# Attention feeding an ELU feed-forward layer: the Tile scheduler's order of the engines exchanged for one written by hand

## The chip, the cores and the metric

The kernel runs on one core of a Trainium2 chip. The metric is the device time of one execution in microseconds (us), the median of several runs. The core has five engines with an instruction stream each: TensorE (PE) multiplies matrices and writes to PSUM, VectorE (DVE) and ScalarE (ACT) work element by element, GpSimd (POOL) does too and issues transfers from a software queue, and SyncE (SP) issues transfers from a hardware queue. An engine works its stream in order; engines wait for each other by semaphores.

## The reference, cut to what matters

There are 8 batches of 8 heads, 576 queries and keys of 64 elements, and 16 beacon keys and values per batch in front of them. All inputs and the output are float32.

```python
k_all = np.concatenate([beacon_k, k], axis=2)      # 16 + 576 = 592 keys
v_all = np.concatenate([beacon_v, v], axis=2)
scores = scale * np.matmul(q, k_all.transpose(0, 1, 3, 2))
scores = np.where(causal, -1000000000.0, scores)   # beacons are seen by all
a = np.exp(scores - scores.max(-1, keepdims=True))
a /= a.sum(-1, keepdims=True) + 1e-09
attn = np.matmul(a, v_all)                         # (8, 8, 576, 64)
x = attn.transpose(0, 2, 1, 3).reshape(4608, 512)
h = x @ w_in                                       # 512 -> 2048
g = np.where(h > 0.0, h, np.exp(np.minimum(h, 0.0)) - 1.0)
out = g @ w_out                                    # 2048 -> 512
```

## The kernel before

Attention goes by batch and by pair of heads (`emit_pair`, 32 of them). Queries and keys arrive as bfloat16 with the token on the partition, are transposed on PE (`tq`, `tk`) and copied by ACT to `qT` and `kT`, in which the two heads of a pair lie on partitions 0 to 63 and 64 to 127. For each of five chunks of 128 keys and each head, PE computes a strip of scores with the keys on the partitions (`stp`), for the queries from `ilo` on that may see the chunk: 576, 464, 336, 208 and 80 columns. ACT takes the exponential to `et` (10 activations for a pair), and DVE multiplies the diagonal block with a triangle. Then PE sums over the keys, for query columns 0 to 511 and 512 to 575 apart: values times weights to `u_ps` and, with a block of ones, the row sums to `l_ps`. ACT forms the reciprocal of the row sums as exp(-ln(l)), in two activations (`rl`, L243 and L244), and DVE multiplies it in (`xallT`, L245).

The feed-forward layer goes by tiles of 512 tokens, nine of them (`gen_moe_tile`). FFN1 has 16 chunks of four matmuls of 512 columns (`hps`); each chunk goes through an exponential on ACT (`e_sb`), a maximum on DVE (`r_sb`) and a combination on DVE (`gt`). FFN2 has four output blocks of 16 matmuls (`ops`), each copied by DVE to `osb` and stored by SP. A tile is cut into eight steps; after each pair of heads up to three steps of the tile at hand are put into the program, if its tokens are complete. What is left when the attention is done runs behind it, with other PSUM buffers.

Loads: q and k come by casting transfers that POOL issues, one for each 128 tokens, with 256-byte rows (64 float32). v comes uncast by SP and is cast by POOL. The two weight matrices come uncast by SP in 32 pieces and are cast by DVE. The Tile framework orders the instructions of each engine by priority and puts in the semaphores.

Of the kernel before, what the change touches and what calls it, by code (L numbers as in the profile page):

```python
# [12 lines left out]
ALU = mybir.AluOpType  # L14


def _ceildiv(a, b):
    return (a + b - 1) // b
# [3 lines left out]
def kernel(  # L22
# [57 lines left out]
    konst = ctx.enter_context(tc.tile_pool(name="konst", bufs=1))  # L80
    big = ctx.enter_context(tc.tile_pool(name="big", bufs=1))
    astage = ctx.enter_context(tc.tile_pool(name="astage", bufs=2))
    attn = ctx.enter_context(tc.tile_pool(name="attn", bufs=2))
    melt = ctx.enter_context(tc.tile_pool(name="melt", bufs=3))
    gpool = ctx.enter_context(tc.tile_pool(name="gpool", bufs=18))
    opool = ctx.enter_context(tc.tile_pool(name="opool", bufs=2))

    ident = konst.tile([P, P], FP32)
    make_identity(nc, ident)
    identb = konst.tile([P, P], BF16)  # L90
    make_identity(nc, identb)
    triu32 = konst.tile([P, P], FP32)
    nc.gpsimd.memset(triu32, 1.0)
    nc.gpsimd.affine_select(
        out=triu32,
        in_=triu32,
        compare_op=ALU.is_ge,
        fill=0.0,
        base=0,
        pattern=[[1, P]],  # L100
        channel_multiplier=-1,
    )
# [5 lines left out]
    w_out16 = big.tile([P, NFC, DM], FP16)

    def load_batch_stage(b):  # L110
        qst = astage.tile([P, NQT, H, D], BF16, tag="qst")
        kst = astage.tile([P, NKC, H, D], BF16, tag="kst")
        vst32 = astage.tile([P, NKC, H, D], FP32, tag="vst32", bufs=1)
        for sti in range(NQT):
            n = q_tsz[sti]
            nc.gpsimd.dma_start(  # L116
                out=qst[0:n, sti, :, :],
                in_=q[b, :, P * sti:P * sti + n, :].rearrange("h s d -> s h d"),
            )
        for (src, bsrc, dst, eng) in ((k, beacon_k, kst, nc.gpsimd), (v, beacon_v, vst32, nc.sync)):  # L120
            eng.dma_start(
                out=dst[0:NB, 0, :, :],
                in_=bsrc[b, :, :, :].rearrange("h n d -> n h d"),
            )
            for jc in range(NKC):
                lo = max(0, P * jc - NB)
                r0 = NB if jc == 0 else 0
                n = kc_sz[jc] - r0
                eng.dma_start(  # L129
                    out=dst[r0:r0 + n, jc, :, :],  # L130
                    in_=src[b, :, lo:lo + n, :].rearrange("h s d -> s h d"),
                )
        v16 = astage.tile([P, NKC, H, 2, D], FP16, tag="v16")
        for jc in range(NKC):
            n = kc_sz[jc]
            nc.gpsimd.tensor_copy(out=v16[0:n, jc, :, 0, :], in_=vst32[0:n, jc, :, :])
        nc.gpsimd.memset(v16[:, :, :, 1, :], 1.0)
        v16f = v16.rearrange("p nkc h two d -> p nkc (h two d)")
        return qst, kst, v16f

    def emit_weights():
        CH = 512
        with tc.tile_pool(name="wstage", bufs=3) as wstage:
            for cc in range(NCC):
                for fo in range(0, DF, CH):
                    wst = wstage.tile([P, CH], FP32, tag="w_st")
                    nc.sync.dma_start(out=wst, in_=moe_w_in[cc * P:(cc + 1) * P, fo:fo + CH])
                    nc.vector.tensor_copy(out=w_in16[:, cc, fo:fo + CH], in_=wst)  # L148
            for fc in range(NFC):
                wst = wstage.tile([P, DM], FP32, tag="w_st")  # L150
                nc.sync.dma_start(out=wst, in_=moe_w_out[fc * P:(fc + 1) * P, :])
                nc.vector.tensor_copy(out=w_out16[:, fc, :], in_=wst)
# [97 lines left out]
    def gen_moe_tile(psum, tt):  # L250
        gts = []
        for fc in range(NFC):
# [18 lines left out]
            if fc % 4 == 3:  # L271
                yield
# [20 lines left out]
    with tc.tile_pool(name="psumI", bufs=1, space=bass.MemoryType.PSUM) as psumI:  # L293
# [3 lines left out]
        for b in range(B):  # L297
            if b + 1 < B:
                stages[b + 1] = load_batch_stage(b + 1)
# [50 lines left out]
```

## Time and profile before

| what | value |
|---|---|
| median of 3 runs | 537.46 us (536.59 to 537.99) |
| span of the profiled execution | 535.9 us |
| PE busy | 472.3 us, 88% of the span, 3392 matmuls |
| DVE busy | 315.4 us, 59% |
| ACT busy | 288.0 us, 54% |
| POOL busy | 117.7 us, 22% |
| moved by DMA | 37.66 MB in 124649 packets, mean 70 GB/s |

The profile gives the profiled execution by its span alone, the time from its first to its last instruction; what lies around the span is read from the timed runs, whose median is 1.6 us above it. Matmuls are pipelined and their ends are modelled, so the busy time of PE counts overlaps and the start-to-start distance of two matmuls tells their cost. In a row of the timeline the first number is the start, the second the time to the end of the last instruction of the row; a bracket gives the idle time of the engine before it and what ended it. The transfer sizes of the casting queue count the bytes written.

### The profile page before, as it was taken

The page shows a single profiled execution, that of the slowest core. Times are in us where ns is not written, and L with a number is a line of the kernel's source. Part 1 is how long each engine was busy: PE and PEld are TensorE (multiplying, and loading weights), DVE is VectorE, ACT ScalarE, POOL GpSimd, SP SyncE. Part 2 cuts the span into 40 slices and gives each one's busy share as a digit, 9 for nine tenths or more (in the row PEclk, how much of TensorE's full clock was granted, in tenths as well). Part 3 has the DMA queues.
Part 4 walks back from the last instruction along what each step waited for, and adds up shares of the span by engine and source line. Part 5 has one row for each costly group of instructions (what it writes and reads, how often), then busy time and mean ns, then how long its engine had stood idle before and what let it go on. Part 6 is the DMA issues. An engine that isn't in the chain of part 4 may idle for free.

```text
span 535.9 us, 8863 instructions
## 1 busy us (share of the span) xinstructions
PE 472.3 (88%) x3392; PEld 210.9 (39%) x3392; DVE 315.4 (59%) x741; ACT 288.0 (54%) x657; POOL 117.7 (22%) x146
## 2 busy tenths in 40 slices
PE   0268898999999999999999999999999999689997
PEld 0023333444444444444444444444444444234442
DVE  0533336667566656665666646665665466449594
ACT  0224555678357836783577457844775577224150
POOL 8912064025300630064006300640000000000000
PEclk9999999999999999999999999999999999999999
DMA  9995596319510941094109420911001100110202
GB/s 172 184 199 148 148 203 146 63 11 81 131 39 1 91 125 45 2 91 117 55 0 91 100 72 1 89 41 41 1 0 40 40 2 1 39 40 0 80 0 79
DMA packets 124649, 37.66 MB, mean 70 GB/s; under 512 B 115904, under 2 KB 115904, under 8 KB 124608
## 3 DMA queue, kind: packets, MB, share of 16 engines
q0 software_dynamic: 76160, 9.57, 28.1%
q1 hardware_dynamic: 48448, 27.53, 18.5%
q8 instruction: 26, 0.43, 0.3%
q14 instruction: 15, 0.12, 0.1%
HBM read 37.22 MB, written 9.44 MB: 87 GB/s over the span
## 4 chain that ended last, share of the span: by engine, by line
PE 70%; ACT 14%; DVE 7%; issue 4%; DMA 3%; SPq 1%; DVEq 0%
PE hps L255 22%; PE ops L276 21%; PE stp L191 9%; PE u_ps L232 7%; PE l_ps L237 7%; ACT e_sb L263 6%; DMA wst<-in_moe_w_in_dram 3%; ACT rl L243 3%; DVE r_sb L265 2%; PE tq L159 2%; PE tk L170 1%; DVE w_in_96 L148 1%; ACT kT L176 1%; DVE osb L284 1%; SPq L129 1%
## 5 line engine op out<-in xcount | busy, mean ns | idle before, releaser
L276 PE MATMUL ops<-w_out_97,gt 128*128 128x512 f16 x576 | 147.8, 380 | 4.2 <-DVE osb L284 2.3
L265 DVE TENSOR_SCALAR r_sb<-hps 128x512 f16<-128x512 f32 x144 | 98.1, 689 | 88.8 <-ACT e_sb L263 88.8
L263 ACT ACTIVATE e_sb<-hps 128x512 f32<-128x512 f32 x144 | 86.2, 599 | 91.6 <-PE hps L255 69.1
L267 DVE SCALAR_TENSOR_TENSOR gt<-e_sb,r_sb 128x512 f16<-128x512 f32 x144 | 98.9, 695 | 1.3
L191 PE MATMUL stp<-qT,kT 64*128 64x64 bf16 (+6 forms) x640 | 81.0, 253 | 12.1 <-ACT kT L176 2.0
L276 PEld LDWEIGHTS <-gt 128*128 128x128 f16 x576 | 55.2, 97 | 71.6 <-issue 6.7
L116 POOL DMA_DIRECT2D qst<-in_q_dram x40 | 33.8, 865 | 176.2 <-PE tq L159 143.3
L255 PEld LDWEIGHTS <-w_in_96 128*128 128x128 f16 x576 | 49.5, 98 | 57.7 <-issue 12.2
L191 PEld LDWEIGHTS <-kT 64*128 64x128 bf16 (+1 forms) x640 | 32.1, 100 | 94.0 <-issue 83.2
L284 DVE COPY osb<-ops 128x512 f32<-128x512 f32 x36 | 24.7, 690 | 59.5 <-PE ops L276 59.4
L255 PE MATMUL hps<-xallT_92,w_in_96 128*128 128x512 f16 x144 | 56.0, 389 | 4.0 <-DVE r_sb L265 2.7
L255 PE MATMUL hps<-xallT_94,w_in_96 128*128 128x512 f16 x144 | 55.3, 384 | 0.0
L255 PE MATMUL hps<-xallT_93,w_in_96 128*128 128x512 f16 x144 | 55.3, 384 | 0.0
L255 PE MATMUL hps<-xallT_95,w_in_96 128*128 128x512 f16 x144 | 55.1, 382 | 0.0
L243 ACT ACTIVATE rl<-l_ps 128x512 f32<-128x512 f32 x64 | 26.3, 411 | 33.3 <-PE l_ps L237 33.1
L159 PE MATMUL tq<-identb,qst 128*128 128x128 bf16 (+1 forms) x160 | 21.3, 229 | 16.8 <-DMA qst<-in_q_dram 14.7
L165 ACT COPY qT<-tq 128x576 bf16<-128x576 bf16 x32 | 20.5, 640 | 26.2 <-PE tq L159 26.2
L129 POOL DMA_DIRECT2D kst<-in_k_dram x40 | 33.9, 893 | 2.9 <-DMA qst<-in_q_dram 2.7
L244 ACT ACTIVATE rl<-rl 128x512 f32<-128x512 f32 x64 | 29.0, 453 | 0.7
L148 DVE CAST w_in_96<-wst 128x512 f16<-128x512 f32 x16 | 12.0, 766 | 20.3 <-DMA wst<-in_moe_w_in_dram 20.3
L176 ACT COPY kT<-tk 128x592 bf16<-128x592 bf16 x32 | 21.2, 662 | 3.4 <-PE tk L170 3.4
L159 PEld LDWEIGHTS <-qst 128*128 128x128 bf16 (+1 forms) x160 | 12.2, 99 | 25.9 <-DMA qst<-in_q_dram 15.4
(372 smaller groups left out, 643.4 us busy)
## 6 DMA issues: line engine op xcount, KB each, us to landing
out_dram<-osb SPq DMA_DIRECT2D x36, 256.0 KB, 2.0
qst<-in_q_dram POOLq DMA_DIRECT2D x32, 128.0 KB, 4.5
wst<-in_moe_w_in_dram SPq DMA_DIRECT2D x16, 256.0 KB, 5.7
wst<-in_moe_w_out_dram SPq DMA_DIRECT2D x16, 256.0 KB, 2.9
kst<-in_k_dram POOLq DMA_DIRECT2D x24, 128.0 KB, 4.4
kst<-in_k_dram POOLq DMA_DIRECT2D x8, 112.0 KB, 4.4
vst_103<-in_v_dram SPq DMA_DIRECT2D x3, 256.0 KB, 5.9
vst_230<-in_v_dram SPq DMA_DIRECT2D x3, 256.0 KB, 3.6
```

What stands on the lines that cost most here:

```text
L116: nc.gpsimd.dma_start(out=qst[0:n, sti, :, :], in_=q[b, :, P * sti:P * sti + n, :].rearrange("h s d -> s h d"),)
L129: eng.dma_start(out=dst[r0:r0 + n, jc, :, :], in_=src[b, :, lo:lo + n, :].rearrange("h s d -> s h d"),)
L159: nc.tensor.transpose(out=tq[:, P * sti:P * sti + n], in_=qst[0:n, sti, ha:ha + 2, :], identity=identb[0:n, 0:n],)
L191: nc.tensor.matmul(out=stp[0:njc, a:bb], lhsT=kT[dlo:dlo + 64, P * jc:P * jc + njc], rhs=qT[dlo:dlo + 64, a:bb], start=True, stop=True,)
L232: nc.tensor.matmul(out=u_ps[dlo:dlo + 64, a - ba:w], lhsT=v16f[0:njc, jc, c0:c0 + D], rhs=mv, start=first, stop=last, skip_group_check=True,)
L237: nc.tensor.matmul(out=l_ps[dlo:dlo + 64, a - ba:w], lhsT=v16f[0:njc, jc, c0 + D:c0 + 2 * D], rhs=mv, start=first, stop=last, skip_group_c ...
L243: nc.scalar.activation(out=rl[:, 0:w], in_=l_ps, func=AFT.Ln, bias=0.0, scale=1.0)
L255: nc.tensor.matmul(out=hps, lhsT=w_in16[:, cc, P * fc:P * fc + P], rhs=xallT[cc][:, TTS * tt:TTS * (tt + 1)], start=(cc == 0), stop=(cc == ...
L263: nc.scalar.activation(out=e_sb, in_=hps, func=AFT.Exp, bias=0.0, scale=1.0)
L265: nc.vector.tensor_scalar(out=r_sb, in0=hps, scalar1=0.0, scalar2=None, op0=ALU.max)
L267: nc.vector.scalar_tensor_tensor(out=gt, in0=e_sb, scalar=1.0, in1=r_sb, op0=ALU.subtract, op1=ALU.min)
L276: nc.tensor.matmul(out=ops, lhsT=gts[fc][:, P * tc_:P * (tc_ + 1)], rhs=w_out16[:, fc, :], start=(fc == 0), stop=(fc == NFC - 1),)
```

## The change

All five engines now run in program order (`manual_schedule`). The program goes in 11 periods. Period p holds the attention of batch p (p up to 7), the FFN1 of tile p-1 and the FFN2 of tile p-2, cut into 16 turns: a turn has one FFN1 chunk (four matmuls), four FFN2 matmuls, and one slot of attention, if there is one left. A pair of heads takes three slots: two score groups; two more score groups; the transposes of the next pair (`T`) and the sums over the keys (`AV`). The last slots of a batch are `AV` of the last pair with `AVR` (query columns 512 to 575 of all four pairs at once), and `T` of the next batch's first pair.

The scores of both heads are packed: the 1664 columns of a head's five strips are cut into four groups of 416, one PSUM tile of two banks holds a group of both heads, and one activation of 832 columns takes its exponential (4 instead of 10 for a pair). All attention tiles share one PSUM tag `S` with two buffers; `hps` and `ops` have two buffers each. Masks are multiplied for both heads at once. The reciprocal is taken by DVE (`nc.vector.reciprocal`, 512 columns for a pair, and 256 once for a batch) in the place of ACT's two activations. The copy of `ops` to `osb` moves from DVE to ACT. Transposes are 24 of 96 columns for a pair, since q and k are loaded with six consecutive tokens on a partition, rows of 1536 bytes; the beacon keys are transposed once and copied into each `kT` by POOL. All loads, v and the weights too, are casting transfers that POOL issues, in the order of the program; DVE's and POOL's casts of weights and v are gone.

```diff
--- before.py
+++ after.py
+    NP = H // 2
+    R = 6
...
+    NG = 4
+    GW = ECOLS // NG
+    assert GW * NG == ECOLS and GW <= 512
+    Q1 = 512
...
+    psum = ctx.enter_context(tc.tile_pool(name="psum", bufs=2, space=bass.MemoryType.PSUM))
+    ctx.enter_context(tc.manual_schedule(
+        engines={ENG.PE, ENG.Activation, ENG.DVE, ENG.Pool, ENG.SP}))
...
+    def load_qk(b, h0, h1):
+        for src, dst in ((q, st[b][0]), (k, st[b][1])):
+            nc.gpsimd.dma_start(
+                out=dst[:, h0:h1, :, :].rearrange("p h r d -> p h (r d)"),
+                in_=src[b, h0:h1, :, :].rearrange("h (p r) d -> p h (r d)", r=R),
+            )
+
+    def load_v(b):
+        v16 = st[b][2]
+        nc.gpsimd.dma_start(
+            out=v16[0:NB, 0, :, :], in_=beacon_v[b].rearrange("h n d -> n h d"))
+        for j in range(NKC):
+            r0 = NB if j == 0 else 0
+            n = kc[j] - r0
+            nc.gpsimd.dma_start(
+                out=v16[r0:r0 + n, j, :, :],
+                in_=v[b, :, ilo[j]:ilo[j] + n, :].rearrange("h s d -> s h d"),
...
+    new_stage(0)
+    load_qk(0, 0, 2)
...
+    for b in range(B):
+        nc.gpsimd.dma_start(
+            out=bkst[NB * b:NB * (b + 1), :, :],
+            in_=beacon_k[b].rearrange("h n d -> n h d"))
+    load_qk(0, 2, 4)
...
+    load_v(0)
+    load_qk(0, 4, 8)
+    for cc in range(NCC):
+        nc.gpsimd.dma_start(out=w_in16[:, cc, :], in_=moe_w_in[cc * P:(cc + 1) * P, :])
+    wo_v = moe_w_out.rearrange("(f p) m -> p f m", p=P)
+    for f0 in range(0, NFC, 4):
+        nc.gpsimd.dma_start(out=w_out16[:, f0:f0 + 4, :], in_=wo_v[:, f0:f0 + 4, :])
...
+    def beacon_T():
+        tb = psum.tile([P, 2, 1024], BF16, tag="S", name="tb")
+        for p in range(NP):
+            nc.tensor.transpose(
+                out=tb[:, 0, P * p:P * (p + 1)], in_=bkst[:, 2 * p:2 * p + 2, :], identity=identb)
+        nc.vector.tensor_copy(out=bkT, in_=tb[:, 0, 0:NP * P])
...
+    def T(b, p):
+        qst, kst, _ = st[b]
+        t = psum.tile([P, 2, 1024], BF16, tag="S", name="tp")
+        for i, src in ((0, qst), (1, kst)):
+            for r in range(R):
+                for h in range(2):
+                    nc.tensor.transpose(
+                        out=t[D * h:D * (h + 1), i, PR * r:PR * (r + 1)],
+                        in_=src[:, 2 * p + h, r, :],
+                        identity=identb[0:PR, 0:PR],
+                    )
+        qT = attn.tile([P, S], BF16, tag="qT")
+        kT = kTs[(b * NP + p) % NKT]
+        nc.gpsimd.tensor_copy(out=kT[:, 0:NB], in_=bkT[:, p, NB * b:NB * (b + 1)])
+        nc.scalar.copy(
+            out=qT.rearrange("c (p r) -> c p r", r=R),
+            in_=t[:, 0, 0:S].rearrange("c (r p) -> c p r", r=R))
+        nc.scalar.copy(
+            out=kT[:, NB:SK].rearrange("c (p r) -> c p r", r=R),
+            in_=t[:, 1, 0:S].rearrange("c (r p) -> c p r", r=R))
+        qkT[(b, p)] = (qT, kT)
...
+    def SC(b, p, g):
+        qT, kT = qkT[(b, p)]
+        if g == 0:
+            ets[(b, p)] = attn.tile([P, 2, ECOLS], FP16, tag="et", bufs=6, name="et")
+        et = ets[(b, p)]
+        s = psum.tile([P, 2, 512], FP32, tag="S", name="sc")
+        c0, c1 = GW * g, GW * (g + 1)
+        masks = []
+        for j in range(NKC):
+            a, e = max(c0, eoff[j]), min(c1, eoff[j + 1])
+            if a >= e:
+                continue
+            qa = a - eoff[j] + ilo[j]
+            for h in range(2):
+                nc.tensor.matmul(
+                    out=s[:, h, a - c0:e - c0],
+                    lhsT=kT[D * h:D * (h + 1), P * j:P * (j + 1)],
+                    rhs=qT[D * h:D * (h + 1), qa:qa + e - a],
+                    start=True, stop=True, skip_group_check=True,
                 )
+            if a == eoff[j]:
+                masks.append(j)
+        nc.scalar.activation(
+            out=et[:, :, c0:c1], in_=s[:, :, 0:GW], func=AFT.Exp, bias=0.0, scale=SCALE)
+        for j in masks:
+            t0 = NB if j == 0 else 0
+            w = min(P, S - ilo[j]) - t0
+            o = et[0:kc[j], :, eoff[j]:eoff[j] + w]
+            nc.vector.tensor_tensor(
+                out=o, in0=o, in1=triu[0:kc[j], :, t0:t0 + w], op=ALU.mult)
+    def av_mms(b, p, qa, qe, u, l, first):
+        v16 = st[b][2]
+        et = ets[(b, p)]
+        for j in range(NKC):
+            a = max(qa, ilo[j])
+            if a >= qe:
+                continue
+            ca = eoff[j] + a - ilo[j]
+            ce = ca + qe - a
+            for dst, isl in ((u, False), (l, True)):
+                for h in range(2):
+                    nc.tensor.matmul(
+                        out=dst[D * h:D * (h + 1), a - qa:qe - qa],
+                        lhsT=ones[0:kc[j], :] if isl else v16[0:kc[j], j, 2 * p + h, :],
+                        rhs=et[0:kc[j], h, ca:ce],
+                        start=(first and j == 0),
+                        stop=(j == NKC - 1 or ilo[j + 1] >= qe),
+                        skip_group_check=True,
                     )
+    def AV(b, p):
+        a = psum.tile([P, 2, 512], FP32, tag="S", name="av")
+        av_mms(b, p, 0, Q1, a[:, 0, 0:Q1], a[:, 1, 0:Q1], True)
+        rl = attn.tile([P, 512], FP32, tag="rl")
+        nc.vector.reciprocal(out=rl[:, 0:Q1], in_=a[:, 1, 0:Q1])
+        nc.vector.tensor_tensor(
+            out=xT[:, p, b * S:b * S + Q1], in0=a[:, 0, 0:Q1], in1=rl[:, 0:Q1], op=ALU.mult)
+    def AVR(b):
+        a = psum.tile([P, 2, 512], FP32, tag="S", name="avr")
+        for p in range(NP):
+            av_mms(b, p, Q1, S, a[:, 0, QR * p:QR * (p + 1)], a[:, 1, QR * p:QR * (p + 1)], p == 0)
+        w = NP * QR
+        rl = attn.tile([P, 512], FP32, tag="rl")
+        nc.vector.reciprocal(out=rl[:, 0:w], in_=a[:, 1, 0:w])
+        nc.vector.tensor_tensor(
+            out=xT[:, :, b * S + Q1:(b + 1) * S],
+            in0=a[:, 0, 0:w].rearrange("c (p q) -> c p q", p=NP),
+            in1=rl[:, 0:w].rearrange("c (p q) -> c p q", p=NP), op=ALU.mult)
+    def slots_of(b):
+        sl = []
+        for p in range(NP):
+            sl.append(lambda p=p: (SC(b, p, 0), SC(b, p, 1)))
+            sl.append(lambda p=p: (SC(b, p, 2), SC(b, p, 3)))
+            if p + 1 < NP:
+                sl.append(lambda p=p: (T(b, p + 1), AV(b, p)))
+            else:
+                sl.append(lambda p=p: (AV(b, p), AVR(b)))
+        if b + 1 < B:
+            sl.append(lambda: T(b + 1, 0))
+        return sl
+    gts = {}
+    def ffn1(t, fc):
+        hps = psum.tile([P, TT], FP32, tag="hps", name="hps")
+        for cc in range(NCC):
+            nc.tensor.matmul(
+                out=hps, lhsT=w_in16[:, cc, P * fc:P * (fc + 1)],
+                rhs=xT[:, cc, TT * t:TT * (t + 1)],
+                start=(cc == 0), stop=(cc == NCC - 1))
+        e = melt.tile([P, TT], FP32, tag="e")
+        nc.scalar.activation(out=e, in_=hps, func=AFT.Exp, bias=0.0, scale=1.0)
+        r = melt.tile([P, TT], FP16, tag="r")
+        nc.vector.tensor_scalar(out=r, in0=hps, scalar1=0.0, scalar2=None, op0=ALU.max)
+        gt = gpool.tile([P, TT], FP16, tag="g", name="gt")
+        nc.vector.scalar_tensor_tensor(
+            out=gt, in0=e, scalar=1.0, in1=r, op0=ALU.subtract, op1=ALU.min)
+        gts[(t, fc)] = gt
+    cur_ops = [None]
+    def ffn2(t, i):
+        tb, f0 = (i * FPS) // NFC, (i * FPS) % NFC
+        if f0 == 0:
+            cur_ops[0] = psum.tile([P, DM], FP32, tag="ops", name="ops")
+        ops = cur_ops[0]
+        for fc in range(f0, f0 + FPS):
+            nc.tensor.matmul(
+                out=ops, lhsT=gts[(t, fc)][:, P * tb:P * (tb + 1)], rhs=w_out16[:, fc, :],
+                start=(fc == 0), stop=(fc == NFC - 1))
+        if f0 + FPS == NFC:
+            osb = melt.tile([P, DM], FP32, tag="osb")
+            nc.scalar.copy(out=osb, in_=ops)
+            row = t * TT + tb * P
+            nc.sync.dma_start(out=out[row:row + P, :], in_=osb)
+    beacon_T()
+    T(0, 0)
+    for period in range(NTT + 2):
+        b, t1, t2 = period, period - 1, period - 2
+        if b + 1 < B:
+            new_stage(b + 1)
+            load_qk(b + 1, 0, H)
+            load_v(b + 1)
+        sl = slots_of(b) if b < B else []
+        if t1 < 0:
+            for s in sl:
+                s()
+            continue
+        for i in range(NFC):
+            if t1 < NTT:
+                ffn1(t1, i)
+            if t2 >= 0:
+                ffn2(t2, i)
+            if i < len(sl):
+                sl[i]()
```

## Rows read from the trace of the kernel before

**Rows 1.** Windows: three stretches; busy time of each engine, clock, DMA share, GB/s.
```profile
0.00:94.00 94.00, 59.74 (x344) 23.35 (x345) 36.13 (x93) 35.28 (x81) 46.70 (x61) 1.00 1.11 171
94.00:460.00 366.00, 345.27 (x2745) 158.15 (x2744) 230.82 (x569) 233.44 (x546) 71.00 (x85) 1.00 0.38 50
460.00:480.00 20.00, 15.32 (x75) 6.55 (x69) 6.38 (x11) 2.21 (x5) 0.00 (x0) 1.00 0.14 53
```
**Rows 2.** Chain that ended last, in order of time: start, duration, what.
```profile
213.67 1.20 issue
...
251.09 3.45 PE ops L276 x16
...
432.26 1.19 issue
```
**Rows 3.** Groups of instructions, shapes apart: busy us, mean ns of one | idle before.
```profile
L276 PE MATMUL ops<-w_out_97,gt 128*128 128x512 f16 x576 | 147.8, 380 | 4.2 <-DVE osb L284 2.3 <-DVE gt L267 1.6
L267 DVE SCALAR_TENSOR_TENSOR gt<-e_sb,r_sb 128x512 f16<-128x512 f32 x144 | 98.9, 695 | 1.3
L265 DVE TENSOR_SCALAR r_sb<-hps 128x512 f16<-128x512 f32 x144 | 98.1, 689 | 88.8 <-ACT e_sb L263 88.8
L263 ACT ACTIVATE e_sb<-hps 128x512 f32<-128x512 f32 x144 | 86.2, 599 | 91.6 <-PE hps L255 69.1 <-DVE gt L267 11.2 <-issue 10.1
L245 DVE TENSOR_TENSOR xallT_94<-u_ps,rl 128x512 f16<-128x512 f32 x8 | 5.5, 692 | 3.3 <-ACT rl L244 3.3
L245 DVE TENSOR_TENSOR xallT_93<-u_ps,rl 128x64 f16<-128x64 f32 x8 | 1.7, 216 | 0.8 <-PE u_ps L232 0.8
L136 POOL CAST v_121<-vst_103 80x512 f16<-80x512 f32 x1 | 2.9, 2891 | 0.0
```
**Rows 4.** Timeline of PE in the steady part.
```profile
203.55 0.38 PE L255 MATMUL hps<-xallT_95,w_in_96 128*128 128x512 f16 x1
203.86 0.22 PE L237 MATMUL l_ps<-et_2304,v_1518 128*64 128x64 f16 x1
...
204.01 0.20 PE L237 MATMUL l_ps<-et_2305,v_1518 80*64 80x64 f16 x1
204.14 0.53 PE L159 MATMUL tq<-identb,qst 128*128 128x128 bf16 x5
204.60 0.43 PE L170 MATMUL tk<-identb,kst 128*128 128x128 bf16 x5
...
209.48 0.40 PE L232 MATMUL u_ps<-et_2556,v_1518 128*64 128x512 f16 x1
209.49 0.40 PE L232 MATMUL u_ps<-et_2557,v_1518 128*64 128x512 f16 x1
209.72 0.38 PE L237 MATMUL l_ps<-et_2556,v_1518 128*64 128x512 f16 x1
```
**Rows 5.** Timeline of all engines at the start.
```profile
3.09 3.34 POOL L116 DMA_DIRECT2D qst<-in_q_dram  x4
6.92 2.63 POOL L129 DMA_DIRECT2D kst<-in_k_dram  x3
10.20 0.29 PE L159 MATMUL tq<-identb,qst 128*128 128x128 bf16 x1 [2.47 <-DMA qst<-in_q_dram]
10.44 0.88 POOL L129 DMA_DIRECT2D kst<-in_k_dram  x1 [0.89 <-DMA qst<-in_q_dram]
11.23 0.29 PE L159 MATMUL tq<-identb,qst 128*128 128x128 bf16 x1 [0.75 <-DMA qst<-in_q_dram]
11.47 0.73 POOL L129 DMA_DIRECT2D kst<-in_k_dram  x1 [0.16 <-issue]
...
32.94 0.63 PE L237 MATMUL l_ps<-et_271,v_121 128*64 128x512 f16 x1
```
**Rows 6.** Timeline of ACT in the steady part.
```profile
207.22 0.65 ACT L198 ACTIVATE et_2556<-stp 128x576 f16<-128x576 f32 x1
207.75 0.66 ACT L198 ACTIVATE et_2557<-stp 128x576 f16<-128x576 f32 x1
...
212.40 0.34 ACT L198 ACTIVATE et_2556<-stp 128x208 f16<-128x208 f32 x1
212.62 0.35 ACT L198 ACTIVATE et_2557<-stp 128x208 f16<-128x208 f32 x1
```
**Rows 7.** Timeline of DVE in the steady part.
```profile
221.97 0.22 DVE L213 TENSOR_TENSOR et_2761<-et_2761,triu_90 128x128 f16<-128x128 f16 x1
222.11 0.22 DVE L213 TENSOR_TENSOR et_2760<-et_2760,triu_90 128x128 f16<-128x128 f16 x1
```
**Rows 8.** The page's table of DMA queues.
```profile
q0 software_dynamic: 76160, 9.57, 28.1%
```

More of the change, by code (lines that the diff above doesn't have):

```diff
@@ L14 @@
 ALU = mybir.AluOpType
[L17 to L18 removed]
+ENG = mybir.EngineType
 @with_exitstack
@@ L78 @@
     )
[L80 to L88, printed above, removed]
@@ L108 @@
[L108 to L131, printed above, removed]
-                )
[L133 to L152, printed above, removed]
@@ L289 @@
-    stages = {}
-    next_tt = 0
-    HPSB = {"psumI": 1, "psumT": 4}
-    OPSB = {"psumI": 1, "psumT": 4}
-    with tc.tile_pool(name="psumI", bufs=1, space=bass.MemoryType.PSUM) as psumI:
-        stages[0] = load_batch_stage(0)
-        emit_weights()
-        dripper = None
-        for b in range(B):
-            if b + 1 < B:
-                stages[b + 1] = load_batch_stage(b + 1)
-            qst, kst, v16f = stages.pop(b)
-            for hp in range(HPB):
-                emit_pair(psumI, b, hp, qst, kst, v16f)
-                for _ in range(3):
-                    if dripper is None:
-                        if next_tt < NTT and TTS * (next_tt + 1) <= S * b:
-                            dripper = gen_moe_tile(psumI, next_tt)
-                            next_tt += 1
-                        else:
-                            break
-                    if next(dripper, StopIteration) is StopIteration:
-                        dripper = None
-        if dripper is not None:
-            for _ in dripper:
-                pass
@@ L315 @@
-    with tc.tile_pool(name="psumT", bufs=1, space=bass.MemoryType.PSUM) as psumT:
-        while next_tt < NTT:
-            for _ in gen_moe_tile(psumT, next_tt):
-                pass
-            next_tt += 1
+    bkst = konst.tile([P, H, D], BF16)
+    for b in range(B):
[3 more added lines that the diff above has]
+    load_qk(0, 2, 4)
+    triu = konst.tile([P, 2, P], FP16)
+    nc.gpsimd.memset(triu, 1.0)
@@ new lines @@
+    bkT = konst.tile([P, NP, P], BF16)
+    def beacon_T():
[4 more added lines that the diff above has]
+        nc.vector.tensor_copy(out=bkT, in_=tb[:, 0, 0:NP * P])
+    NKT = 3
+    kTs = [konst.tile([P, P * NKC], BF16, name=f"kT{i}") for i in range(NKT)]
+    for kt in kTs:
+        nc.gpsimd.memset(kt[:, SK:P * NKC], 0.0)
```

203 lines of the change are left out of this document (39 added, 164 removed).

## The prediction

> **What bounds the kernel now.** I read the busy time by stretches first [rows 1]. Up to 94 us the DMA share is over one (two queues at once) and PE is busy 59.7 of 94 us: the kernel is loading, and does little but the attention of two batches. From 94 to 460 us PE is busy 345 of 366 us, DVE 231 and ACT 233; then come 76 us of feed-forward work alone. The middle is PE's: sixteen FFN2 matmuls follow each other in 3.45 us, 0.216 us each [rows 2]. The reader should trust this distance and not the 380 ns of a matmul's row [rows 3], in which pipelined ends overlap. The chain repeats one stall of 1.20 us from batch to batch; its first and last occurrences, four batches apart, give (432.26 - 213.67)/4 = 54.6 us a batch [rows 2]. A batch carries 1.125 tiles, 1.125 x 128 x 0.216 = 31.1 us of FFN, so attention takes 23.5 us of PE's time there. The columns need far less, as the sum below shows.
>
> One thing is not where the page shows it. The granted clock reads 1.00 in all stretches [rows 1], but a 512-column matmul of the row sums takes 0.63 us at 33 us and 0.38 us in the steady part [rows 4, 5]: by its durations PE ran at the lower of its two levels (1.2 GHz) in the sparse beginning.
>
> **What a period costs PE.** FFN1 and FFN2 of one tile each are 128 x 0.216 = 27.6 us. In attention two heads run at the same time: two 512-column matmuls start 0.01 us apart and the next comes 0.23 us later [rows 4], 0.45 ns for a column of both. Scores have 1664 columns, 0.75 us a pair; the sums over the keys up to query 511 have 2 x 1344, 1.2 us. Fewer score matmuls with the same columns save no more than starts. Transposes: 24 of 96 columns in the place of ten. Ten take 0.46 us for each five before [rows 4]; bounds for the new ones are 12 x 0.043 = 0.5 us, if two heads overlap, and 24 x 0.092 = 2.2 us, if none does; I take 0.8, near the overlapping rows. Together 2.75 us a pair, 11.0 a batch. AVR is 40 couples of 64 columns; five such couples start within 0.15 us [rows 4], 0.037 each: 1.5 us. Passing from FFN to attention costs 0.31 - 0.216 = 0.095 us [rows 4]; 24 such passages are 2.3 us. The sum is 27.6 + 11.0 + 1.5 + 2.3 = 42.4 us, against 54.6.
>
> **What the other engines carry in it.** On ACT, 368 columns more cost 0.31 us more from start to start [rows 6], so an activation of 832 columns takes 0.53 + 0.22 = 0.75 us. A period has 16 of these, 16 FFN exponentials and 4 output copies near 0.5, and 8 transposed copies at 0.54: 12 + 10 + 4.3 = 26 us. ACT takes on the output copies and loses the logarithms, and is covered by PE either way. DVE has 32 passes of 0.69 [rows 3], 22 us, 20 masks of two heads near 0.2 [rows 7], 4 us, 3 us of multiplications, and the reciprocals. Casts of v and weights that go from POOL and DVE save nothing: both engines wait there.
>
> **The reciprocal.** No row shows one. Call X the time of 512 columns. From below it is an ordinary DVE pass, 0.69 us; the slowest pass over 512 columns in the trace is a POOL cast of 2.89 us [rows 3]. An exact quotient isn't one step of arithmetic, as the fast rows are, so I take the upper one, 2.9. DVE's period then is 22 + 4 + 3 + 4.5 x 2.9 = 42 us, still under PE's with its waits. But X also stands in a chain. `S` has two buffers; `AV`'s is free only when the reciprocal and the multiplication have read it, 0.2 + X + 0.65 us after its last matmul, and the second score group of the next pair needs it. Behind that group in PE's order stand the next FFN1 and FFN2. PE has 1.73 us of FFN, 0.19 of the first group and 0.2 of passages to fill the time: it stalls X - 1.25 = 1.65 us, three times a batch. After the last pair `T` of the next batch waits likewise, with AVR as more cover: 0.45 us. Period: 42.4 + 3 x 1.65 + 0.45 = 47.8 us.
> The Trainium skill ("VectorE: DVE Perf Modes", "First, the fixed hardware budget") says that the reciprocal is an iterative divide with a repeat count of 8. No run here shows it; if it means eight passes, the result is the slower rival below, and if it means one step of an eight-stage pipe, the fast one.
>
> **The start.** POOL never has more than eight casting transfers under way before: it issues nine, the first having landed; the tenth waits until 10.44 us, when PE has just begun on the second piece of q (10.20), the eleventh follows the third in the same way (11.23, 11.47) [rows 5]. Now weights, v and all else go through this queue in the program's order, and the transfers of batch 1 (the 29th to 36th) stand ahead of the copy of the beacon keys into the second pair's `kT`, on POOL. The 36th waits for the 28th, the last piece of w_out. So the second pair's scores, and everything behind them on PE, wait until all weights have landed.
> When is that? The queue wrote 9.57 MB in 28.1% of 535.9 us [rows 8], 63.5 KB/us, in rows of 128 bytes; the 2 KB rows of the output moved 53 GB/s at a share of 0.14 [rows 1], 379 KB/us. v and the beacons, 0.74 MB written, keep short rows: 11.6 us. q and k (1.18 MB written, 2.36 read) get longer rows: 6.2 to 18.6 us, weights (4.19 written, 8.39 read) 22 to 66 us. Neither row is nearer, casting on one side and length on the other; I take the geometric middles, 10.7 and 38. With 3 us ahead: 3 + 11.6 + 10.7 + 38 = 63 us; the ends are 43 and 99.
>
> **The sum.** Three pairs of batch 0 remain, without FFN and at the low clock: 3.7 us to the fourth exponential, 0.8 for masks and the last transposes, 2.4 for the sums at twice 1.2, 0.2 and X: 7.1 + X = 10.0 each, and 3 for AVR: 33 us. Period 1 has FFN1 only, 0.86 us a turn; ACT paces a pair at 6.0 us, the stall is X - 0.25, so 4 x 8.65 + 5.2 for four turns without slots + 1.2 = 41 us. Periods 2 to 7: 6 x 47.8 = 287. Periods 8 to 10: 27.6 + 27.6 + 13.8 = 69, and 3.5 for the last copy and store. 63 + 33 + 41 + 287 + 72.5 = 496.5 us of span, against 535.9; with the 1.6 us that the median lies above the span, **498 us**.
>
> **Rivals.**
> *The reciprocal is an ordinary pass.* X = 0.69 removes the stalls: start 63, batch 0 25, period 1 32, 6 x 42.4 = 254, and 72.5: 446.5, so 448 us. For it: every DVE row over 512 columns costs 0.69, whatever the operation. Against it: none of them divides.
> *The reciprocal sets the pace, and the kernel is slower.* Between 64 and 512 columns a DVE pass grows by 476 ns [rows 3], 0.54 us per 512 columns; an iterative divide costs that several times. Each us of X costs 27 us in the six periods, 4 in period 1 and 3.5 in batch 0, some 34. From X = 4.1 on the time passes 537. At eight passes, 0.15 + 8 x 0.54 = 4.5, DVE alone has 49 us in a period, the chain gives 42.4 + 3 x 3.25 + 2.05 and 0.6 for an FFN1 held by its PSUM buffer, 54.8; 63 + 38.6 + 47.4 + 329 + 72.5 = 550.5, so 552 us.
> *POOL's queue doesn't hold the second pair.* Then batch 0 starts near 25 us and is done at 68 in the place of 96, the weights being there at 63: 470 us. Against it: the waits of [rows 5].
> *Weights move as slowly as short rows.* They land at 99 us: 534 us, the change's gain lost in the load.
>
> **How the numbers follow.** Forecast 0.38 (its own range 475 to 525), ordinary pass 0.24, paced by the reciprocal 0.20, no hold 0.10, slow weights 0.08. The range reaches from the ordinary pass with fast weights, 430, to eight passes, 555. Within 0.3%, about what a measurement of this kernel can tell from no change, lies 0.04, from the last case and the forecast's upper edge; faster is 0.76 and slower 0.20.
>
> **What would show it.** The row of the reciprocal gives X at once. The waits should name DVE's product into `xT` as what PE's second score group waits for, by X - 1.25. POOL's `kT` copy of the second pair should start when the last weights have landed, and PE idle until then. Two periods, from one first FFN1 chunk to the next, should lie 47.8 us apart, and the last two near 27.6. The prediction fails if heads don't overlap in the new transposes (six us a batch more), if the idle beginning lasts longer, or if PE falls back to the low level in the stalls.

## The result and the profile after

The changed kernel takes 471.55 us (median, 469.05 to 472.52) beside 537.46 us: 0.876 of the time before, with an interval of 0.873 to 0.880. The forecast was 498 us in a range of 430 to 555. The profiled execution has a span of 467.2 us.

The page of the changed kernel: head, busy time, granted clock, the casting queue, the group of the reciprocal.
```profile
span 467.2 us, 8876 instructions
PE 377.9 (81%) x3716; PEld 189.4 (41%) x3716; DVE 372.1 (80%) x529; ACT 245.8 (53%) x373; POOL 69.1 (15%) x128
PEclk9995678998999999999999999999999999999999
q0 software_dynamic: 55104, 18.62, 35.9%
L243 DVE RECIPROCAL rl<-av 128x512 f32<-128x512 f32 x32 | 107.4, 3355 | 10.6 <-PE av L230 10.3
```
The first line to read is PE's. Before, PE was busy 472.3 us of a span of 535.9 and idle for 63.6; now it is busy for 377.9 and idle for 89.3. So the change took 94 us of busy time from PE and gave 26 us of idle time back: 68.7 us, the whole difference of the spans.

Where the work went shows in the windows of one period: four batches of before (start and end are those of the stalls in [rows 2]), and one period of the changed kernel. The columns are those of [rows 1].
```profile
213.67:432.26 218.59, 207.07 (x1634) 94.82 (x1634) 136.46 (x337) 137.26 (x320) 42.69 (x51) 1.00 0.37 48
```
```profile
157.86:204.42 46.56, 42.08 (x448) 20.89 (x448) 43.64 (x63) 28.96 (x44) 6.97 (x12) 1.00 0.44 62
```
Before, PE had 207.07/4 = 51.8 us of work in a batch of 54.65; one tile's FFN1 and FFN2 are 27.6 of them, so attention cost 24.2. Now it is 42.08 - 27.6 = 14.5. Work fell by 9.7 us, idle time rose from 2.9 to 4.5, and the period is 8.1 us shorter. Note DVE: 43.64 us, more than PE; before it was 34.1.

Which part of attention got cheaper can be read by lines, with the caution that overlapping lines are counted twice. The sums over the keys are L232 and L237 before and L230 now, in four batches each:
```profile
213.67:432.26 218.59, 35.31 (x320) 1.00 0.37 48
213.67:432.26 218.59, 35.81 (x320) 1.00 0.37 48
```
```profile
203.35:389.61 186.26, 26.64 (x640) 1.00 0.29 45
```
The same 640 matmuls are busy for 26.6 us in the place of 71.1, 6.7 a batch in the place of 17.8 (the two lines of before overlap each other). Scores fall from 9.3 to 4.8 us a batch and transposes from 4.0 to 2.6.

What PE waits for in such a period, from its timeline (a wait stands in brackets), and DVE's rows beside it:
```profile
167.72 0.45 PE L172 MATMUL tp<-identb,qst 96*64 96x96 bf16 x12
168.00 0.42 PE L172 MATMUL tp<-identb,kst 96*64 96x96 bf16 x12
168.25 0.38 PE L230 MATMUL av<-et,v_1198 128*64 128x512 f16 x2
...
171.36 0.35 PE L202 MATMUL sc<-qT,kT_126 64*128 64x416 bf16 x2
172.87 0.35 PE L202 MATMUL sc<-qT,kT_126 64*128 64x160 bf16 x4 [1.16 <-ACT et L210]
...
201.80 0.45 PE L172 MATMUL tp<-identb,qst 96*64 96x96 bf16 x12 [1.31 <-DVE xT L244]
```
```profile
169.63 3.36 DVE L243 RECIPROCAL rl<-av 128x512 f32<-128x512 f32 x1 [0.19 <-PE av L230]
173.03 0.69 DVE L244 TENSOR_TENSOR xT<-av,rl 128x512 f16<-128x512 f32 x1
```
The second score group starts at 172.87, before DVE has finished with `AV`'s buffer (173.72). So it isn't that buffer which it takes: `AV` keeps one of the two `S` buffers for as long as the reciprocal lasts, and both score groups go through the other one, the second waiting for the exponential of the first. That is 1.0 to 1.2 us, three times a period; once a period, for 1.31 us, `T` of the next batch does wait for DVE's product.

The start: POOL's timeline, PE's timeline, and the chain of waits of the changed kernel.
```profile
20.54 0.74 POOL L147 DMA_DIRECT2D w_out_81<-in_moe_w_out_dram  x1 [1.31 <-DMA qst<-in_q_dram]
24.49 0.79 POOL L106 DMA_DIRECT2D qst<-in_q_dram  x1 [1.28 <-DMA w_in_80<-in_moe_w_in_dram]
...
43.06 0.74 POOL L118 DMA_DIRECT2D v_168<-in_v_dram  x1 [2.44 <-issue]
43.79 0.21 POOL L179 COPY kT_126<-bkT 128x16 bf16<-128x16 bf16 x1
```
```profile
23.26 0.88 PE L202 MATMUL sc<-qT,kT_125 64*128 64x416 bf16 x6 [12.37 <-POOL kT_125 L179]
...
44.05 0.88 PE L202 MATMUL sc<-qT,kT_126 64*128 64x416 bf16 x6 [14.35 <-POOL kT_126 L179]
...
51.87 0.35 PE L202 MATMUL sc<-qT,kT_127 64*128 64x160 bf16 x4 [0.96 <-ACT et L210]
...
59.33 0.35 PE L202 MATMUL sc<-qT,kT_125 64*128 64x160 bf16 x4 [0.96 <-ACT et L210]
```
```profile
22.04 19.96 DMA w_out_81<-in_moe_w_out_dram
```
The second pair's scores wait 14.35 us for a 0.21 us copy on POOL, which stands behind batch 1's issues, and those behind the weights, landed at 42.0. In the order of the program the 27th transfer (issued at 20.54) waits for the 19th and the 29th (24.49) for the 21st, so eight are under way. The first pair waits too, 12.37 us, for its own copy behind the issues of the weights. After the second pair, a pair takes 59.33 - 51.87 = 7.46 us.

### The profile page after: what moved, and what is told of

Its sections match the earlier page's. It is cut to its first block, busy times and chain, and to the rows that moved or that the text cites. A ratio compares the mean times of both kernels' runs of the same rounds, so it can differ in the third digit from the quotient of the medians.

```text
span 467.2 us, 8876 instructions
## 1 busy us (share of the span) xinstructions
PE 377.9 (81%) x3716; PEld 189.4 (41%) x3716; DVE 372.1 (80%) x529; ACT 245.8 (53%) x373; POOL 69.1 (15%) x128
## 4 chain that ended last, share of the span: by engine, by line
PE 55%; DVE 28%; DMA 6%; ACT 6%; POOL 3%; issue 2%; ACTq 0%; POOLq 0%
PE ops L299 21%; PE hps L278 20%; DVE rl L243 12%; PE av L230 6%; DVE r L285 5%; PE sc L202 5%; DVE gt L287 4%; DMA w_out_81<-in_moe_w_out_dram 4%; ACT et L210 4%; PE tp L172 3%; DVE xT L244 3%; DVE rl L253 2%; DVE et L216 2%; DMA kst<-in_k_dram 1%; POOL v_84 L118 1%
## 5 line engine op out<-in xcount | busy, mean ns | idle before, releaser
L278 PE MATMUL hps<-xT,w_in_80 128*128 128x512 f16 x576 | 150.4, 384 | 3.8 <-DVE r L285 3.2
L283 ACT ACTIVATE e<-hps 128x512 f32<-128x512 f32 x144 | 86.4, 600 | 100.5 <-PE hps L278 70.4
L210 ACT ACTIVATE et<-sc 128x832 f16<-128x832 f32 x128 | 106.3, 864 | 59.9 <-PE sc L202 59.9
L243 DVE RECIPROCAL rl<-av 128x512 f32<-128x512 f32 x32 | 107.4, 3355 | 10.6 <-PE av L230 10.3
L285 DVE TENSOR_SCALAR r<-hps 128x512 f16<-128x512 f32 x144 | 98.9, 687 | 14.2 <-ACT e L283 12.4
L287 DVE SCALAR_TENSOR_TENSOR gt<-e,r 128x512 f16<-128x512 f32 x144 | 99.6, 692 | 7.4
L216 DVE TENSOR_TENSOR et<-et,triu 128x256 f16<-128x256 f16 (+2 forms) x160 | 38.0, 272 | 35.3 <-ACT et L210 34.4
L230 PE MATMUL av<-et,ones 128*64 128x512 f16 (+4 forms) x320 | 39.2, 295 | 0.0
L202 PE MATMUL sc<-qT,kT_125 64*128 64x208 bf16 (+5 forms) x176 | 14.5, 265 | 24.6 <-POOL kT_125 L179 12.4
L202 PE MATMUL sc<-qT,kT_126 64*128 64x208 bf16 (+5 forms) x176 | 14.6, 272 | 24.1 <-POOL kT_126 L179 14.3
L230 PEld LDWEIGHTS <-ones 128*64 128x64 f16 (+1 forms) x640 | 31.3, 117 | 5.6 <-issue 0.8
L202 PE MATMUL sc<-qT,kT_127 64*128 64x208 bf16 (+5 forms) x160 | 12.7, 257 | 10.7 <-ACT et L210 10.2
```

Source lines behind the costliest of these rows:

```text
L202: nc.tensor.matmul(out=s[:, h, a - c0:e - c0], lhsT=kT[D * h:D * (h + 1), P * j:P * (j + 1)], rhs=qT[D * h:D * (h + 1), qa:qa + e - a], st ...
L210: nc.scalar.activation(out=et[:, :, c0:c1], in_=s[:, :, 0:GW], func=AFT.Exp, bias=0.0, scale=SCALE)
L216: nc.vector.tensor_tensor(out=o, in0=o, in1=triu[0:kc[j], :, t0:t0 + w], op=ALU.mult)
L230: nc.tensor.matmul(out=dst[D * h:D * (h + 1), a - qa:qe - qa], lhsT=ones[0:kc[j], :] if isl else v16[0:kc[j], j, 2 * p + h, :], rhs=et[0:k ...
L243: nc.vector.reciprocal(out=rl[:, 0:Q1], in_=a[:, 1, 0:Q1])
L278: nc.tensor.matmul(out=hps, lhsT=w_in16[:, cc, P * fc:P * (fc + 1)], rhs=xT[:, cc, TT * t:TT * (t + 1)], start=(cc == 0), stop=(cc == NCC ...
```

## The experiments

Theory: the middle gains because PE's attention work shrinks and FFN turns cover the waits that are left; reciprocal and POOL order give part of it back. Rivals, run by run: the gain comes from the loads, from the packed activation, or from the order written by hand.

**The reciprocal.** `e_nodiv` puts an ordinary pass in its place, in the pair (shown) and in `AVR`: the output lacks the division by the row sums.
```diff
-        nc.vector.reciprocal(out=rl[:, 0:Q1], in_=a[:, 1, 0:Q1])
+        nc.vector.tensor_scalar(out=rl[:, 0:Q1], in0=a[:, 1, 0:Q1], scalar1=1e-5, scalar2=None, op0=ALU.mult)
```


> The reciprocal is left out: DVE multiplies the row sums by 1e-5 in its place, so the output is not the reference's; everything else stays. A DVE pass over 512 columns costs 0.69 us, against 3.36 for the reciprocal. Theory P (the reciprocal costs only where PE waits for it, at the end of a batch, and in batches 0 and 1 where little hides it): the period falls from 46.6 by the two waits behind AVR, 2.5 us, to 44; batch 0 loses 3 x 2.7 + 2 and period 1 some 8; 471.6 - 15 - 10 - 8 gives about 438 us. Theory D (DVE, busy 43.7 of 46.6 us, sets the pace): DVE then has 32 us in a period, PE's own 41 to 42 us set it, and the time is 471.6 - 30 - 18, about 424 us. The reciprocal hidden: no change, 470.

`e_lnexp` takes it as before, by two ACT activations, both in the pair (shown) and in `AVR`, with the logarithm in ACT's table set:
```diff
-        nc.vector.reciprocal(out=rl[:, 0:Q1], in_=a[:, 1, 0:Q1])
+        nc.scalar.activation(out=rl[:, 0:Q1], in_=a[:, 1, 0:Q1], func=AFT.Ln, bias=0.0, scale=1.0)
+        nc.scalar.activation(out=rl[:, 0:Q1], in_=rl[:, 0:Q1], func=AFT.Exp, bias=0.0, scale=-1.0)
```


> The reciprocal goes back to ACT, as exp(-ln(l)) in two activations like in the kernel before; all else stays. X becomes about 1.25 us and moves from DVE (43.7 us a period) to ACT (29.0 us, plus 5). Theory P: period 44.5, batch 0 and period 1 shorter by 2.1 a pair, about 440 us. Theory D: period near 42, about 426 us. If ACT's longer queue delays the exponentials on which PE's second score group already waits 1.0 us, the period stays at 46 and the time at 455.

Measured: 421.62 us (0.785, 0.783 to 0.788) and 426.82 us (0.795, 0.792 to 0.798). One period of each, in this order:
```profile
174.49:215.82 41.33, 41.33 (x450) 20.83 (x448) 33.01 (x62) 28.20 (x44) 7.49 (x13) 1.00 0.50 70
```
```profile
176.04:217.78 41.74, 41.74 (x458) 20.89 (x455) 29.63 (x58) 33.66 (x54) 7.47 (x12) 1.00 0.50 69
```
PE is busy from end to end of both. So the waits on the exponential and on `xT` are the reciprocal's doing, and it costs 46.56 - 41.33 = 5.2 us a period, and 50 us in all. Theory P is refuted: it let the three waits on the exponential stand. The times are those of Theory D, but they don't prove that DVE's pace sets the period, since both edits free the `S` buffer early and relieve DVE at once. The rows above speak for the buffer: PE's three waits end with an exponential, and DVE has 2.9 us without work in the period.

**POOL's order.** `e_kt_dve` lets DVE copy the beacon keys, and leaves POOL the issues.
```diff
-        nc.gpsimd.tensor_copy(out=kT[:, 0:NB], in_=bkT[:, p, NB * b:NB * (b + 1)])
+        nc.vector.tensor_copy(out=kT[:, 0:NB], in_=bkT[:, p, NB * b:NB * (b + 1)])
```


> Only the copy of the beacon keys into kT moves from POOL to DVE. Theory: the 14.4 us in which PE waits for POOL's second kT copy come from POOL's order (36 transfers, eight under way, ahead of that copy); they go, and the second pair follows the first at about 30 us; 14 us less at most, 458 us, a little more if period 1 then waits for batch 1's q and k. Rival: the data itself is late (v of batch 0 or the weights), PE waits somewhere else at the start, and the time stays at 468 or above.

Measured: 456.48 us (0.850, 0.847 to 0.853), 15 us less. PE's timeline of this run shows the long wait gone and other, shorter ones:
```profile
22.59 0.25 PE L202 MATMUL sc<-qT,kT 64*128 64x80 bf16 x2 [8.01 <-POOL kT L162]
26.22 0.53 PE L202 MATMUL sc<-qT,kT 64*128 64x416 bf16 x2
...
53.57 0.69 PE L172 MATMUL tp<-identb,qst 96*64 96x96 bf16 x12 [2.98 <-DMA qst<-in_q_dram]
```
The 8.01 us of the first pair are POOL's order again: the memset of the last columns of `kT` (L162) still stands behind the issues of the weights.

**The loads alone.** `b_cast` is the kernel before with v and weights as casting transfers, without the casts on POOL and DVE, and with nothing else of the change.
```diff
-        vst32 = astage.tile([P, NKC, H, D], FP32, tag="vst32", bufs=1)
+        v16 = astage.tile([P, NKC, H, 2, D], FP16, tag="v16")
...
+        for cc in range(NCC):
+            nc.gpsimd.dma_start(out=w_in16[:, cc, :], in_=moe_w_in[cc * P:(cc + 1) * P, :])
...
+        for f0 in range(0, NFC, 4):
+            nc.gpsimd.dma_start(out=w_out16[:, f0:f0 + 4, :], in_=wo_v[:, f0:f0 + 4, :])
```


> The kernel before with one part of the change alone: v and the weights come by POOL's casting queue (the weights in eight pieces, rows of 2 KB and more), and the casts on DVE and POOL go. Theory (the middle of the kernel, its 54.6 us a batch, is where the change gains, the start only helps): batch 0's short rows take 31 us in the queue, the weights 20 (the measure of the changed kernel, 22 to 42 us), batch 1's q and k 25 more, so FFN can begin near 75 to 80 us in the place of 88; 8 to 13 us less, 525 to 530 us. Rival (the loads carry half of the gain or more): 505 us or less.

Measured: 522.19 us (0.972, 0.968 to 0.976), 15 us less, beside 66 by the whole change. Its windows beside [rows 1]: up to 94 us PE has 74.26 us of work in the place of 59.74, and the middle is as before.
```profile
0.00:94.00 94.00, 74.26 (x455) 29.71 (x456) 25.09 (x85) 45.37 (x103) 54.26 (x72) 1.00 1.16 103
94.00:460.00 366.00, 343.29 (x2689) 157.38 (x2688) 218.26 (x553) 224.44 (x525) 79.43 (x90) 1.00 0.45 46
```

**Cover by FFN turns.** `e_apart` gives all attention slots of a period ahead of its FFN turns.
```diff
+        for s in sl:
+            s()
         for i in range(NFC):
...
-            if i < len(sl):
-                sl[i]()
```


> The alternation is undone: in each period all attention slots stand ahead of the sixteen FFN turns; nothing else changes. Theory I (the gain of the middle comes from FFN turns that cover attention's chains on ACT and DVE): a pair without FFN took 7.46 us in batch 0 of the changed kernel, so a period becomes 4 x 7.5 + 6 for the rest and 27.6 of FFN, some 63 us in the place of 46.6; six of these and some 15 us for period 1 give 471.6 + 98 + 15, about 585 us, above the kernel before. Rival (the cheaper attention, with 41 us of PE work a period in all, is what counts, and the engines' queues overlap the two parts by themselves): not above 490 us.

Measured: 578.22 us (1.076, 1.071 to 1.081), 107 us more than the change. A window from one batch's `AVR` to the next, and PE's timeline where the FFN turns begin again:
```profile
224.61:288.17 63.56, 50.85 (x451) 27.35 (x450) 44.80 (x62) 30.49 (x46) 6.47 (x12) 0.82 0.32 45
```
```profile
225.84 1.91 PE L299 MATMUL ops<-w_out,gt 128*128 128x512 f16 x4
227.54 1.90 PE L278 MATMUL hps<-xT,w_in 128*128 128x512 f16 x4
229.25 1.05 PE L299 MATMUL ops<-w_out,gt 128*128 128x512 f16 x4
```
Idle time is 12.7 us in the place of 4.5, and PE's work 50.9 in the place of 42.1. The latter goes with the clock: after attention with its waits the same four FFN matmuls take 1.9 us for some microseconds, and then 1.05, the lower and the higher of the two levels; the granted clock of the period is 0.82. The FFN rows lose only some 2.5 of the 8.8 us by it (three groups 1.7 us apart in the place of 0.86). The larger part is in attention itself, as the clock of a stretch of it shows:
```profile
260.00:280.00 20.00, 11.58 (x136) 7.70 (x137) 14.37 (x19) 11.78 (x16) 1.74 (x3) 0.67 0.37 53
```

**Second buffers of `hps` and `ops`.** The packed attention tiles leave PSUM for them. `e_single` takes them away, in the changed kernel:
```diff
-        hps = psum.tile([P, TT], FP32, tag="hps", name="hps")
+        hps = psum.tile([P, TT], FP32, tag="hps", name="hps", bufs=1)
...
-            cur_ops[0] = psum.tile([P, DM], FP32, tag="ops", name="ops")
+            cur_ops[0] = psum.tile([P, DM], FP32, tag="ops", name="ops", bufs=1)
```


> The changed kernel with one PSUM buffer each for hps and ops, as the kernel before has beside attention, in the place of two. The maximum of an FFN1 chunk is done 1.4 us after its last matmul, and PE has 0.86 us of FFN2 and 0.5 to 1.8 us of a slot in between: little is lost where there is a slot, 0.5 us in turns without one (three a period, all 32 of the tail's: 17 us), and behind a reciprocal, 4 us, PE stands about 2 us, four times a period. Theory (the second buffers that packing attention's PSUM makes room for are a main source of the gain): 8 to 10 us a period, 471.6 + 55 + 17, about 540 us. Rival (one buffer suffices where the turns are spaced): the tail's 17 us alone, 489.

Measured: 585.34 us (1.090, 1.085 to 1.095), 114 us more, and far more than forecast. What PE waits for in this run (us in total, times, longest), and one period of it:
```profile
PE hps L278 <- DVE r L285: 78.7, 85, 3.8
PE sc L202 <- ACT et L210: 29.4, 31, 1.2
```
```profile
243.59:301.39 57.80, 45.95 (x448) 22.26 (x448) 44.52 (x62) 29.19 (x45) 7.00 (x13) 0.94 0.36 50
```
A period is 11.2 us longer (forecast 8 to 10), of which 3.9 are PE's work at a granted clock of 0.94. Period 1, for which nothing was counted, is 14 us longer, and the end stage 33, where 17 were counted. An FFN1 chunk must wait until DVE has made `r` of the last one, and `r` stands behind the reciprocal. To part the two, `e_lnexp_kt_single` has the same edit in the kernel without reciprocal and without POOL's copy (`e_lnexp_kt`, below).

> One buffer each for hps and ops, as in the run beside it, but with the reciprocal on ACT and the kT copy on DVE (409.7 us with two buffers). Nothing long stands in DVE's queue now: the cost is 0.5 us in each turn without a slot, 1.5 us a period and 17 in the tail, so about 435 us. If the loss is as large as in the run beside it, it doesn't come from the reciprocal.

Measured: 473.78 us (0.882, 0.879 to 0.885), 64 us above the same kernel with two buffers (409.72): so much the buffers give without the reciprocal. The forecast of 435 was too low here too. PE's timeline in the end stage, where there is no attention:
```profile
422.72 1.02 PE L280 MATMUL hps<-xT,w_in 128*128 128x512 f16 x4 [0.60 <-DVE r L287]
423.58 1.03 PE L301 MATMUL ops<-w_out,gt 128*128 128x512 f16 x4
425.21 1.02 PE L280 MATMUL hps<-xT,w_in 128*128 128x512 f16 x4 [0.60 <-DVE r L287]
```
A turn takes 425.21 - 422.72 = 2.49 us, and 1.73 with two buffers: FFN2's four matmuls don't cover exponential and `r`. The product of batch 7's `AVR` starts at 363.95 us, and 109.0 us are left, where `e_lnexp_kt` has 328.90 and 79.0: 30 of the 64 us are in this stage, where 17 were forecast, and the other 35 ahead of it, where I had counted 1.5 us a period.

**Packing the activation.** `e_unpack` takes the exponential of each head by itself; all else stays.
```diff
-        nc.scalar.activation(
-            out=et[:, :, c0:c1], in_=s[:, :, 0:GW], func=AFT.Exp, bias=0.0, scale=SCALE)
+        for h in range(2):
+            nc.scalar.activation(
+                out=et[:, h, c0:c1], in_=s[:, h, 0:GW], func=AFT.Exp, bias=0.0, scale=SCALE)
```


> The exponential of a score group is taken for each head by itself, two activations of 416 columns in the place of one of 832; matmuls, buffers and order stay. Theory: packing saves a start of 0.06 us each, at most 16 x 0.1 us of ACT a period, which PE doesn't wait for: within 3 us of 471.6. Rival (the packed groups carry a good part of the gain): above 485 us.

Measured: 474.78 us (0.884, 0.879 to 0.889), which overlaps the change's own interval. The medians lie 3.2 us apart: 256 activations of 522 ns in the place of 128 of 864 show no clear cost.

**The copy of `osb`.** `e_osb_dve` moves it back to DVE (`nc.vector.tensor_copy` for `nc.scalar.copy`).

> Only the copy of the FFN2 result goes back from ACT to DVE, four of 0.61 us a period. Theory D (DVE sets the pace): the period grows by 2.4 us, in six periods and a little in the tail: 487 us. Theory P: the period doesn't grow; the exponential that stands behind the copy on ACT comes 0.6 us earlier and PE's wait for it, three times 1.0 us a period, shrinks: 462 to 472 us.

Measured: 478.82 us (0.892, 0.888 to 0.895), 7 us more. Successive products of `AVR` lie 48.5 and 47.2 us apart, in the place of 46.56, in turn: neither the 2.4 us of the one theory nor the gain of the other. DVE's time isn't free any more, but only part of the added work lands on PE.

**The order by hand.** `e_tileorder` removes `manual_schedule`, so that the framework orders the same program.
```diff
-    ctx.enter_context(tc.manual_schedule(
-        engines={ENG.PE, ENG.Activation, ENG.DVE, ENG.Pool, ENG.SP}))
```


> The order by hand is given up: the same program, but the Tile scheduler orders the five engines by its priorities. Theory (the order is the gain, the parts are not): the period goes back towards 54 us and the time to 510 us or more. Rival (the gain is in the program's parts, sums over keys in fewer and packed instructions, and the program text keeps neighbouring work together for the scheduler too): 455 to 480 us.

Measured: 446.32 us (0.831, 0.826 to 0.835): 25 us faster than the order by hand. Both theories missed. Its period:
```profile
238.17:281.41 43.24, 42.15 (x448) 20.72 (x448) 41.71 (x63) 28.67 (x44) 6.98 (x13) 1.00 0.48 67
```
DVE has 41.7 us of work and PE 42.2 in 43.24, so PE's idle time in a period is 1.1 us, where the order by hand leaves 4.5. The start keeps its wait for POOL's copy (14.1 us).

**Together.** `e_lnexp_kt` has the edits of `e_lnexp` and `e_kt_dve`; `e_tile_lnexp_kt` those two and the framework's order.

> Both edits that shortened the time by themselves: the reciprocal on ACT (426.8 us, 44.7 less) and the copy into kT on DVE (456.5 us, 15.1 less). If they act in different places, the one in periods and the other in the wait for POOL at the start, they add up: 471.6 - 44.7 - 15.1, about 412 us. If the faster batch 0 only arrives earlier at the wait for batch 1's q and k (2.98 us in the run with the copy on DVE) the sum loses some 4 us: 416.

> The Tile scheduler's order (446.3 us, batches 43.2 us apart with DVE busy without a gap) with the reciprocal on ACT and the kT copy on DVE (409.7 us in the order by hand, periods of 41.7 us with PE busy without a gap). Theory (once DVE is relieved PE's work sets the middle, and no order can shorten it): 405 to 412 us, the same as by hand. Rival (the order by hand still costs): below 400 us; or the scheduler's order wins only where an engine's queue stalls another, and loses here: above 415.

Measured: 409.72 us (0.762, 0.759 to 0.766) and 405.35 us (0.754, 0.751 to 0.757), the fastest of all. A period of the latter:
```profile
158.26:200.00 41.74, 41.74 (x450) 20.87 (x448) 29.77 (x61) 33.68 (x54) 6.26 (x9) 1.00 0.50 70
```
It is as long as the hand order's with the reciprocal on ACT, 41.74 us: once PE doesn't wait, its work sets the period, whoever wrote the order.

## Why the prediction was right, and where it was off

The direction and the stages held; three sizes were off. By stages, cut at the end of the product of `AVR` (71.2, 110.9 and 390.0 us for batches 0, 1 and 7): batch 0 took 71.2 us (forecast 63 + 33 = 96), six periods 279.1 (287), and period 1 and the end stage together 39.8 + 77.2 = 117.0 (41 + 72.5 = 113.5; together, since the product comes some 4 us before a period ends). The differences, -24.8, -7.9 and +3.5, are the 29 us of span by which it missed.

**The weights' landing was mis-sized.** It was the term with the widest bounds, 43 to 99 us, and I took the geometric middle, 63; it measured 42.0, just beyond the fast end. The window in which they move:
```profile
20.00:40.00 20.00, 5.39 (x60) 3.78 (x60) 5.34 (x7) 4.31 (x6) 6.83 (x13) 0.84 1.15 208
```
208 GB/s for 20 us are the 4.2 MB that w_in and w_out write; their 8.39 MB read make 420 KB/us (at a DMA share of 1.15), beside the 379 of the output's rows from which I had the fast bound. Of the two rows the one of like row length was the nearer, and the casting cost nothing that shows. Choosing the middle cost 19 of the 29 us (the copy into `kT` at 43.8 in the place of 63). What hung on it was right: eight transfers under way, POOL behind them, the second pair behind POOL. `e_kt_dve` shows it by taking the copy from POOL, which saves 15 us, so the rival without a hold is excluded. That the first pair is held too, behind the issues of the weights, was not foreseen.

**The reciprocal was priced near, and its wait was put in the wrong place.** X was taken as 2.9 us and measured 3.36, above the upper bound. From 256 to 512 columns it grows by (3355 - 1747)/256 = 6.3 ns a column (the row of `AVR`'s is below), where [rows 3] give an ordinary pass 476/448 = 1.06.
```profile
L253 DVE RECIPROCAL rl<-avr 128x256 f32<-128x256 f32 x8 | 14.0, 1747 | 0.0
```
The Trainium skill ("VectorE: DVE Perf Modes", "First, the fixed hardware budget") gives its repeat count as 8; the runs show six passes' slope, neither eight nor one. The step that failed is "the second score group of the next pair needs it": by it the period is 42.4 + 3 x (3.36 - 1.25) + 0.9 = 49.6 us at the measured X, and 46.56 was measured. What waits is the group behind the first exponential, because one buffer is left, and its wait is as long as the activation, not as X. Of PE's steps in the steady periods only `T` behind `AVR` waits for DVE's product, 1.31 us, as foreseen. So the slope was wrong too: `e_nodiv` shortens X by some 2.7 us and the kernel by 50, where my sums make it 498 + 0.46 x 34 - 448 = 66. That the forecast of 47.8 us came so near to 46.56 is luck in part: X was taken too small and its wait too long. The same step is behind batch 0: a pair took 7.46 us in the place of 10.0, since its score groups went on, each behind one exponential (0.96), while DVE divided.

**PE's work was near.** `e_nodiv`'s period without any wait is 41.33 us, forecast 42.4. Two heads do overlap in the transposes: from the first of 24 to the next matmul it is 168.25 - 167.72 = 0.53 us (0.8 taken, 0.5 the bound with overlap). One sentence on the kernel before was wrong and entered no sum: a batch there carries one tile, not 1.125 (256 FFN1 matmuls in four batches), so attention had 27.0 us of the interval and not 23.5.

**The rivals.** The ordinary pass was not there, and with it put in (`e_nodiv`) the time is 421.6, 26 us under that rival's 448, of which the landing is 19. The slower rival asked for an X from 4.1 us on, and X is 3.36. Still DVE, with 43.6 us of work, is close to the period of 46.56, and the page's chain names the reciprocal for 14% of the span (`rl`, 12% and 2%). Where the 66 us come from: the loads alone give the kernel before 15 (`b_cast`), and if that adds to the rest, some 51 are the middle's, where PE's attention work is 9.7 us a batch smaller and its idle time 1.6 us larger. The second `hps` and `ops` buffers and the cover by FFN turns are conditions of it: without either the changed kernel is slower than the one before. With the reciprocal on ACT single buffers still leave 474 us, so they decide only together with it. Neither the order by hand, which the title names (the framework's is 25 us faster with this program), nor the one activation for both heads is a source; what the packed PSUM tiles give is the room for the second buffers. By lines the largest fall is in the sums over the keys; which edit took how much of the 9.7 us from PE's attention work (coupled heads in scores, fewer changes between FFN and attention, the transposes) no run here parts.

## What to carry to other kernels

Cut PE's time into work and idle first: the change's gain was work removed, and nearly half of what it could give (62 of the 128 us of `e_lnexp_kt`) was lost to one slow DVE instruction, which held a PSUM buffer, and to a tiny copy behind DMA issues. When a rotating pool is shared by several stages, ask how many buffers are left while the slowest reader holds one, and don't assume which one the next stage takes. When bounds lie far apart, look for the row that shares the property that matters before taking a middle: here it was the length of the rows, not the cast.

## What was unexpected

DVE's reciprocal of 128x512 takes 3.36 us, five times DVE's other passes over 128x512. Casting loads of long rows wrote 208 GB/s at a DMA share of 1.15, 181 KB for each microsecond of a full share, where the casting queue of before wrote 63.5 [rows 8]. With attention alone on PE the granted clock was 0.67 in one stretch of 20 us, and FFN matmuls ran at half speed for some microseconds after it (`e_apart`), a cost of taking work apart that no row of the steady part before showed.
